# Attention and MLP in one kernel on one core: a fifth exp per slot into a stock of tiles before the tail

## The chip, the cores and the metric

One Trainium2 chip, one of its cores. The metric is the device time of one launch in microseconds, of which runs of the kernel before give 1628.36 to 1630.75, median 1630.4. "PE" is TensorE's matmuls, "PEld" its weight loads, "ACT" ScalarE, "DVE" VectorE, "POOL" GpSimd, "SP" the engine whose queue issues nearly all DMAs.

## The reference

The input x is 1 x 2048 x 512; attention has 32 heads of 16, the MLP 1792 hidden units, everything in float32.

```python
xn = _layernorm(x)
q, k, v = split(xn @ wqkv)                 # 32 heads of 16
p = softmax(q @ k.T * 16 ** -0.5)
s = (p @ v) @ wo
r = max(xn @ w1 + b1, 0)
g = silu((r * r) @ w2 + b2)
return x + s * g
```

## The kernel before

**Units, slots and lanes.** Attention is cut into 32 units (8 groups of four heads, times 4 blocks of 512 queries), a unit into 16 slots, one for each block of 128 keys: 512 slots, numbered through, run by one loop at the end of the function. For a slot's keys each of four heads needs one score matmul (`exp_mm`, line 1201, tile `se`, or `pm_t` if "spare") and one exp on ACT (line 1213) into a tile of the ring `pt`. At its end `pv_step` multiplies the exps of the slot two earlier with v into the bank `po` (line 401). Heads 0 and 2 use the upper 64 rows of the matmul array, heads 1 and 3 the lower; these halves are the lanes, and two matmuls on different lanes run side by side.

**Beside the exps.** The softmax needs each row's maximum before its exps. `max_mm` makes score matmuls 24 slots ahead (line 317, tile `pm_t`) and DVE reduces each (line 324). When a unit's maxima are complete, `shift` (lines 366 to 387) turns them on DVE, and DMAs on SP store them to `sh_d` one slot later (`keep`) and load them back into the unit's query tile `qe` (`back`), from where the score matmul subtracts them. The dense work (MLP, then the projection with wo) fills the other lane: `dense()` yields for each slot a list of matmuls, which `slot` interleaves with score matmuls by a string: "s" is an exp's matmul, "m" one for the maximum, "_" an empty place. The other lane's list is `own`.

**The projection.** From slot 454, `wo_part` multiplies 16 tiles of 128 rows with three quarters of wo: two slots each, nine matmuls on lane 0, then nine on lane 1 (line 223), all into the one bank `pd_t`; then ACT copies the bank out (line 736) and POOL gates the copy (lines 737, 738). Two waits bind the lanes: the first matmul of the next tile waits for the copy, and the first matmul of lane 1 waits for `last_use`, the exp or maximum issued last in the slot of lane 0. Per slot there are four exps, those of two key blocks for the two heads of the other lane. In 484 and 485 (PAIR) there are fewer maxima. From 486 (LAST_MAX), the tail, the maxima are through: `wo_last` adds the last quarter, three matmuls a slot, and exps fill the rest, five in one slot and three in the next, to two PSUM pools in turn (`odd`); DVE gates the bank (lines 759, 760).

**The end of a unit.** `evac` copies `po` out on ACT and in six steps, `EVAC` or `EVAC_LAST` slots later, takes the sums by DMA, inverts them (DVE), sends them to DRAM and back (`hl<-r_d`), multiplies and splits (POOL), and stores to `on_d`. Units 30 and 31 are handled on the chip (`unit_inner`, `unit_final`). All five engines follow the order in which the program is written; SP issues its DMAs in that order and stops at the first one that has to wait.

Of the kernel before, what the change touches and what calls it, by code (L numbers as in the profile page):

```python
# [33 lines left out]
NVT = 7  # L34
EVAC = (1, 6, 7, 9, 11, 14)
EVAC_LAST = (1, 3, 4, 5, 7, 9)
# [4 lines left out]
LAST_MAX = 486  # L41
PAIR = (484, 485)
# [12 lines left out]
def kernel(  # L55
# [56 lines left out]
    with ExitStack() as ph:  # L112
# [253 lines left out]
        def shift(u):  # L366
# [14 lines left out]
            def back():  # L381
                for p in range(2):
                    for i in range(2):
                        shift_rows(u, p, i)

# [3 lines left out]
        to_block = []  # L389

# [253 lines left out]
        def wo_pools():  # L644
            wos["f"] = right(wstk, "fp", 4)
            wos["oc1"] = right(wstk, "oc1p", 1)
            tp = tail["p"] = right(wstk, "tailp", 1)
            wos["oc3"] = right(o3, "oc3p", 2)

        def wo_small():  # L650

            tp = tail["p"]
            rows = tp.tile([P, D], F32, name="raw6")
# [3 lines left out]
            raw = tp.tile([P, D], F32, name="raw7")  # L657
            nc.gpsimd.memset(raw, 0.0)
            both = tp.tile([P, D], F32, name="raw67")
# [10 lines left out]
        def wo_load(c, kos):  # L670
            if len(kos) > 1:
                oc = wos["oc3"].tile([P, 2, len(kos), 512], F32R, name="oc")
            else:
                oc = right(wstk, f"oc1{c}p", 1).tile([P, 2, 1, 512], F32R, name="oc") if c else wos["oc1"].tile([P, 2, 1, 512], F32R, name="oc")

            def load(n, ko, a, b):
                nc.sync.dma_start(
                    oc[:, :, n, a:b].bitcast(F32),
                    on_d[ko][:, :, c * 512 + a : c * 512 + b].rearrange("k p t -> p k t"),
                )  # L680
# [10 lines left out]
        def wo_terms(ps, oc, tt, kos):  # L691
            wot = wos["w"]
            ts_ = slice(tt * P, (tt + 1) * P)
            return terms3(ps, [
                (lambda a, q, n=n: oc[q, a, n, ts_], lambda b, q, ko=ko: wot[q, b, ko])
                for n, ko in enumerate(kos)
            ])

        def wo_ask(k):
# [8 lines left out]
            elif c < 2:  # L708
# [6 lines left out]
        def wo_part():  # L715
            for c in range(4):
                for tt in range(4):
# [12 lines left out]
                    if c > 1:  # L730
                        s = tail[c, tt] = tail["p"].tile([P, D], F32, name=f"ts{c}{tt}")
# [3 lines left out]
                    def post():  # L735
# [3 lines left out]
                        if c < 2:  # L739
# [4 lines left out]
        def wo_last(c):  # L744
            for tt in range(4):
# [6 lines left out]
                if k == 18:  # L752
# [33 lines left out]
        def unit_turn(po, i):  # L786

            t = tail["p"].tile([P, 256], F32, name=f"tt{i}")
            nc.vector.transpose(t, po[:, 256 * i : 256 * i + 256])
            sm = tail["p"].tile([P, 8], F32, name=f"tsm{i}")  # L790
            return t.rearrange("p (b r) -> p b r", r=32), sm

        def unit_back(i, rows, sm):
            ot = tail["p"].tile([P, 256], F32, name=f"tot{i}")
# [4 lines left out]
            nc.vector.transpose(ot, rows.rearrange("p b r -> p (b r)"))  # L799
            return ot  # L800
# [38 lines left out]
        def unit_final(po):  # L839
# [5 lines left out]
            hls, ots = [], []  # L845
            for i in range(2):
                ot = unit_back(i, *unit_turn(po, i))
                hl = tail["p"].tile([P, 2, 256], F32R, name=f"thl{i}")
                nc.scalar.activation(hl[:, 0], ot, AF.Copy)
                hls.append(hl)  # L850
                ots.append(ot)

            def low(i):
                nc.vector.tensor_tensor(
                    hls[i][:, 1], ots[i], hls[i][:, 0].bitcast(F32), op=ALU.subtract
                )
# [13 lines left out]
            def add(tt, a, b, eng, queue):  # L870
                g, s = parts[tt]
                eng.tensor_tensor(g[:, a:b], g[:, a:b], s[:, a:b], op=ALU.add)
                queue.dma_start(of[1536 + tt * P : 1536 + (tt + 1) * P, a:b], g[:, a:b])

            low(0)
            for tt, n in ((0, 0), (0, 1), (1, 0), (1, 1), (0, 2), (1, 2)):
                out(tt, n)
            low(1)
            for tt in (2, 3):
                for n in range(3):  # L880
                    out(tt, n)
            gate(0)
            add(0, 0, D, nc.gpsimd, nc.scalar)
            gate(1)
            add(1, 0, D, nc.gpsimd, nc.scalar)
            gate(2)
            gate(3)
            add(2, 0, D, nc.vector, nc.sync)
            add(3, 0, D, nc.vector, nc.sync)

# [522 lines left out]
        def dense():  # L1413
# [12 lines left out]
            for c in range(3):  # L1426
                if c == 0:
                    o3.close()
                    wos["q6"] = right(wstk, "q6p", 1)
                    later(3, lambda: load_q6(3))  # L1430
                yield from wo_last(c)

        odd = itertools.chain((0,) * 4, itertools.cycle((1, 0)))
        flip = [0]
        seen = const.tile([P, 1], F32, name="seen")

        def slot(st, mms, post):
# [4 lines left out]
            for kb in (kb0, kb0 + 1):  # L1442
                pts.setdefault(kb, {})
            spare = st >= LAST_MAX
            ex = [
                lambda j=j, kb=kb: exp_mm(kb, j, pts[kb], spare and next(odd))
                for kb in (kb0, kb0 + 1) for j in (1 - lane, 3 - lane) if j not in pts[kb]
# [15 lines left out]
            if spare and lane == 0:  # L1463

                own.append(lambda: exp_mm(kb0, 0, pts[kb0], next(odd)))
# [11 lines left out]
            other = [None if o == "_" else (ex if o == "s" else mx).pop(0) for o in order]  # L1477
            other[-1:-1] = [None] * (len(own) - len(other))
# [54 lines left out]
        def plain_slot(st):  # L1533

            pts[st] = {}
            for j in range(4):
                exp_mm(st, j, pts[st], next(odd))
# [74 lines left out]
```

## Time and profile before

| | |
|---|---|
| timed runs | 1628.36, 1630.4, 1630.75 us |
| profiled execution | 1627.99 us, span 1626.2 us |
| PE busy | 1610.3 us, 99% of the span |
| DVE, ACT, POOL busy | 1362.1, 1188.9, 520.5 us |
| granted TensorE clock | 0.999 |
| slots 454 to 485 | up to about 1559 us, 3.27 us each |
| slots 486 to 511 | about 1559 to 1614 us |

The page gives the chain that ended last and the costliest groups. Rows of a timeline give the start, the length, the engine, the line, out<-in, the number of merged instructions and, in brackets, the idle time before and what ended it; a row of the windows gives start:end, its length, then busy us and instructions of PE, PEld, DVE, ACT and POOL, the clock, the DMA share and GB/s. An ACT or DVE row of several instructions runs from the first start to the last end.

### The profile page before, as it was taken

What the parts mean: (1) busy time and instruction counts of PE and PEld (TensorE: products, weight loads), DVE (VectorE), ACT (ScalarE), POOL (GpSimd) and SP (SyncE); (2) the same over time, 40 slices, a digit from 0 to 9 for tenths busy, and PEclk for the clock granted to TensorE, in tenths of its full rate; (3) what the DMA queues carried; (4) which work ended last, traced back from release to release, by engine and by line L of the source; (5) the groups of instructions that cost most, each with busy time, mean ns of one, the idle gap of its engine ahead of it and who ended that gap; (6) DMA issues with size and microseconds to landing.
All of it is one profiled execution on the core that took longest, in us unless ns stands there. A gap on an engine that the chain in (4) does not pass through costs nothing.

```text
span 1626.2 us, 36026 instructions
## 1 busy us (share of the span) xinstructions
PE 1610.3 (99%) x13656; PEld 936.1 (58%) x13656; DVE 1362.1 (84%) x2359; ACT 1188.9 (73%) x2349; POOL 520.5 (32%) x547
## 2 busy tenths in 40 slices
PE   8999999999999999999999999999999999999998
PEld 6899665556545654664466456545654565445543
DVE  6486888888888888888888888888888888887744
ACT  7212777777777777877777777777777777777786
POOL 6436667133113310321133112311331133226421
PEclk9999999999999999999999999999999999999999
DMA  8877556434343333434343334423542252247564
GB/s 297 235 236 233 175 162 157 127 96 128 81 103 96 103 88 90 127 87 110 83 119 93 85 87 130 112 68 83 141 112 67 70 155 78 55 126 210 188 179 150
DMA packets 163565, 208.16 MB, mean 128 GB/s; under 512 B 59168, under 2 KB 79136, under 8 KB 161824
## 3 DMA queue, kind: packets, MB, share of 16 engines
q1 hardware_dynamic: 163104, 205.33, 44.6%
q8 instruction: 108, 1.77, 0.5%
q14 instruction: 65, 0.53, 0.1%
q10 hardware_dynamic: 288, 0.52, 0.1%
HBM read 148.64 MB, written 55.56 MB: 126 GB/s over the span
## 4 chain that ended last, share of the span: by engine, by line
PE 98%; DVE 1%; DMA 0%; issue 0%; SPq 0%; DVEq 0%; ACT 0%; ACTq 0%
PE po L401 31%; PE pd_t L255 20%; PE pm_t L317 16%; PE se L1201 14%; PE pd_t L223 7%; PE pm_t L1077 4%; PE pd_t L1077 1%; PE se L1047 1%; PE se L981 1%; PE se L317 1%; PE pm_t L1163 0%; PE pd_t L1047 0%; DVE mx L324 0%; DMA xt<-in_A_x_dram 0%; PE pm_t L1201 0%; PE po L981 0%
## 5 line engine op out<-in xcount | busy, mean ns | idle before, releaser
L324 DVE TENSOR_REDUCE mx<-pm_t 128x1 f32<-128x512 f32 x1927 | 1197.3, 684 | 166.9 <-PE pm_t L317 74.0
L1213 ACT ACTIVATE pt<-se 128x512 f32<-128x512 f32 x1996 | 1035.5, 614 | 252.8 <-PE se L1201 210.4
L317 PE MATMUL pm_t<-ka,qm 64*128 64x512 f32 x1927 | 769.6, 420 | 0.0
L1201 PE MATMUL se<-qe,ka 64*128 64x512 f32 x1996 | 673.0, 396 | 0.3 <-ACT pt L1213 0.3
L401 PE MATMUL po<-pt,v 128*32 128x512 f32 x4096 | 545.3, 604 | 0.2 <-DVE tsm L795 0.2
L317 PEld LDWEIGHTS pm_t<-ka,qm 64*128 64x128 f32 x1927 | 338.3, 184 | 237.0 <-DVE mx L324 225.5
L1201 PEld LDWEIGHTS se<-qe,ka 64*128 64x128 f32 x1996 | 337.2, 184 | 18.1 <-ACT pt L1213 1.7
L255 PEld LDWEIGHTS pd_t<-xc,w1s 64*128 64x128 f32 x2352 | 292.0, 186 | 82.2 <-issue 82.2
L255 PE MATMUL pd_t<-xc,w1s 64*128 64x256 f32 x2352 | 332.2, 288 | 0.0
L255 PE MATMUL pd_t<-w2t,hT 64*128 64x512 f32 x1080 | 300.6, 410 | 0.0
L255 PEld LDWEIGHTS pd_t<-w2t,hT 64*128 64x128 f32 x1080 | 179.0, 184 | 83.2 <-issue 75.5
L555 POOL TENSOR_TENSOR r<-r 128x512 f32<-128x512 f32 x56 | 58.2, 1039 | 370.3 <-ACT r L552 370.3
L401 PEld LDWEIGHTS po<-pt,v 128*32 128x32 f32 x4096 | 81.0, 108 | 159.9 <-issue 136.8
L574 POOL TENSOR_TENSOR u<-u,b_t 128x512 f32<-128x512 f32 x16 | 20.6, 1289 | 320.2 <-ACT u L573 286.3
L324 DVE TENSOR_REDUCE mx<-se 128x1 f32<-128x512 f32 x121 | 77.9, 686 | 26.0 <-PE se L317 26.0
L439 POOL TENSOR_TENSOR ot<-ot,hl 128x512 f32<-128x512 f32 x30 | 38.6, 1286 | 173.9 <-DMA hl<-r_d 132.7
L223 PE MATMUL pd_t<-wot,oc 64*128 64x512 f32 x336 | 90.2, 405 | 0.4 <-issue 0.3
L552 ACT ACTIVATE r<-pd_t,b_t 128x256 f32<-128x256 f32 x112 | 47.0, 470 | 57.0 <-PE pd_t L255 53.8
L223 PEld LDWEIGHTS pd_t<-wot,oc 64*128 64x128 f32 x336 | 58.4, 184 | 46.9 <-ACT pt L1213 12.6
L1077 PE MATMUL pm_t<-xT,wr_t 64*128 64x512 f32 x408 | 73.8, 388 | 0.0
L97 POOL TENSOR_TENSOR hT<-r,hT 128x512 fp32r<-128x512 f32 x56 | 72.3, 1291 | 4.7
L223 PE MATMUL pd_t<-w2t,hT 64*128 64x512 f32 x264 | 68.8, 393 | 0.0
(134 smaller groups left out, 1148.4 us busy)
## 6 DMA issues: line engine op xcount, KB each, us to landing
w1s<-w_d SPq DMA_DIRECT2D x196, 256.0 KB
qm<-q_d SPq DMA_DIRECT2D x384, 32.0 KB
ka<-k_d SPq DMA_DIRECT2D x96, 128.0 KB
qe<-q_d SPq DMA_DIRECT2D x384, 32.0 KB
q_d<-hl SPq DMA_DIRECT2D x16, 512.0 KB
g<-g_d SPq DMA_DIRECT2D x32, 256.0 KB
k_d<-hl SPq DMA_DIRECT2D x15, 512.0 KB
hl<-r_d SPq DMA_DIRECT2D x30, 256.0 KB
```

What stands on the lines that cost most here:

```text
L97: (lo or nc.gpsimd).tensor_tensor(dst[1], raw, dst[0].bitcast(F32), op=ALU.subtract)
L223: mm = nc.tensor.matmul(out_, lh(r), rh(r), start=first_ and lane == 0, stop=last_ and lane == 1, skip_group_check=True,)
L255: mm = nc.tensor.matmul(out_, lh(r), rh(r), start=first_ and lane == 0, stop=last_ and lane == 1, skip_group_check=True,)
L317: nc.tensor.matmul(ps, qms[u][p][64 * j : 64 * j + 64, qb * P : (qb + 1) * P], kas[qd, p][64 * j : 64 * j + 64, kc * 512 : (kc + 1) * 512] ...
L324: return nc.vector.tensor_reduce(mxs[u][:, c, kc : kc + 1], ps, axis=AX.X, op=ALU.max)
L401: nc.tensor.matmul(po[32 * j : 32 * j + 32, :], vs[qd][:, (4 * kb + j) * VW : (4 * kb + j) * VW + 32], pts[j], start=(kb == 0), stop=(kb = ...
L439: nc.gpsimd.tensor_tensor(ot, ot, hl[:, 1].bitcast(F32), op=ALU.mult)
L552: nc.scalar.activation(r[:, i], ps[:, i * CW : (i + 1) * CW], AF.Relu, bias=b1_t[:, fo : fo + 1])
L555: nc.gpsimd.tensor_tensor(r, r, r, op=ALU.mult)
L1077: mm = nc.tensor.matmul(out_, lh(r), rh(r), start=first_ and lane == first, stop=last_ and lane != first, skip_group_check=True,)
L1201: nc.tensor.matmul(se, kas[qd, j // 2][b : b + 64, kb * P : (kb + 1) * P], qes[u][j // 2][b : b + 64, :], start=True, stop=True,)
L1213: return nc.scalar.activation(pts[j], se, AF.Exp, scale=0.25)
```

## The change

From slot 454 on (`RUN`) the exps of a slot are no longer those of its own two key blocks: `run_ahead` hands each lane the next exps in order, five a slot (six in PAIR, three in the tail), as long as their unit's shift has been issued and three tiles stay free. The ring gets 23 more tiles: 3 and 18 new ones and two slices of a v tile that is no longer used. The room comes from `wo_load`, which puts two of its three blocks into the free key tiles `ka`, and from the third row of partial results, which goes through DRAM (`sp_d`) like the first two. The fifth exp is put at the end of the slot's string. A slot without projection matmuls now issues only the exps that are due: none in 502, six in 511.

The rest concerns the tail: unit 31's shift is taken one slot after its maxima, not six; `EVAC_LAST`, which unit 29 alone uses, is shorter; a load of `on_d` is asked for one tile sooner; the last unit's scaling reads `po` again (`unit_scale`), its low parts are made on POOL, and one of the four last additions is done by PE with the identity and ACT.

```diff
+NXR = 18
-EVAC_LAST = (1, 3, 4, 5, 7, 9)
+EVAC_LAST = (1, 2, 2, 3, 4, 6)
+RUN = 454
...
-                late.append((g + (8 if u == 3 else 6 if u else 0), u))
+                late.append((g + {0: 0, 3: 8, NU - 1: 1}.get(u, 6), u))
...
+            more = [left.tile([P, 512], F32, name=f"xl{i}") for i in range(3)]
+            pool = right(wstk, "xpr", 1)
+            more += [pool.tile([P, 512], F32, name=f"xr{i}") for i in range(NXR)]
+            more += [vs["tiles"][0][:, 512 * i : 512 * i + 512] for i in range(2)]
+            rot["pt"] = more + rot["pt"]
...
+                two = rot["ka"][c % 2].rearrange("p (i k n) -> p i k n", i=2, k=2)
+                one = wos["oc3"].tile([P, 2, 512], F32R, name="oc")
+                oc = [two[:, :, 0], two[:, :, 1], one]
...
-                ot = unit_back(i, *unit_turn(po, i))
+                ot = unit_scale(po, i, *unit_turn(po, i))
+                nc.gpsimd.tensor_tensor(hl[:, 1], ot, hl[:, 0].bitcast(F32), op=ALU.subtract)
...
+            for tt in range(4):
+                gate(tt)
+            nc.tensor.matmul(both, ident, parts[1][0], start=False, stop=True)
+            nc.scalar.activation(parts[1][0], both, AF.Copy)
+            add(0, nc.gpsimd)
+            add(2, nc.gpsimd)
+            add(3, nc.vector)
...
+        def run_ahead(st, lane, n, need):
+
+            got = []
+            at = ahead_of.setdefault(lane, 2 * (st - 1))
+            live = sum(len(d) for d in pts.values())
+            while at < 2 * NU * 16:
+                kb, j = at // 2, lane + 2 * (at % 2)
+                if j not in pts.setdefault(kb, {}):
+                    if kb > need and (
+                        len(got) >= n or kb // 16 not in shifted or live + len(got) > len(rot["pt"]) - 3
+                    ):
+                        break
+                    assert kb // 16 in shifted
+                    got.append((kb, j))
+                at += 1
+            ahead_of[lane] = at
+            return got
...
+                n = 3 if spare else 6 if st in PAIR else 5
+                todo = run_ahead(st, 1 - lane, n, st - 1)
...
-            if spare and lane == 0:
-
-                own.append(lambda: exp_mm(kb0, 0, pts[kb0], next(odd)))
...
-                    order = "msmsmsms"
+                    order = "msmsmsms" + "s" * (len(ex) - 4)
...
+            elif k == 0 and not spare:
+                order += "s" * (len(ex) - 4)
             if st in PAIR:
-                order = "sms_s_s_m"
+                order = {5: "smss_ss_m", 6: "smssmss_s"}.get(len(ex), "sms_s_s_m")
...
+            last = st == NU * 16 - 1
+            todo = [run_ahead(st, lane, 0, st if last else st - 1) for lane in range(2)]
```

How it moves instructions is shown at three places; names end in the tile's number. First ACT around a tile's second slot (461), before: four exps (tiles pt0 to pt3), then the copy of `pd_t`, then the next slot's first exp.

```order
L1213 ACTIVATE pt0_1478<-se_21752 128x512 [waits PE_49,Activation_49]
L1213 ACTIVATE pt1_1479<-se_21760 128x512 [waits PE_49,Activation_49]
L1213 ACTIVATE pt2_1480<-se_21768 128x512 [waits PE_49,Activation_49]
L1213 ACTIVATE pt3_1481<-se_21776 128x512 [waits PE_49]
L736 ACTIVATE s_21712<-pd_t_21711 128x512 [waits PE_49]
L1213 ACTIVATE pt4_1482<-se_21805 128x512 [waits PE_49,Activation_49]
```

And ACT at the same place now: five exps (xr0 to xr4) ahead of the copy.

```order
L1232 ACTIVATE xr0_21448<-se_21890 128x512 [waits PE_49]
L1232 ACTIVATE xr1_21449<-se_21898 128x512 [waits PE_49,Activation_49]
L1232 ACTIVATE xr2_21450<-se_21906 128x512 [waits PE_49,Activation_49]
L1232 ACTIVATE xr3_21451<-se_21914 128x512 [waits PE_49]
L1232 ACTIVATE xr4_21452<-se_21922 128x512 [waits PE_49]
L748 ACTIVATE s_21845<-pd_t_21844 128x512
L1232 ACTIVATE xr5_21453<-se_21945 128x512 [waits PE_49,Activation_49]
```

The copy has moved one place back in ACT's queue. Second, PE at the end of a tile's first slot (462) and the start of its second (463), before: `oc` and `wot` are the projection's operands, `po` the four matmuls that end the slot.

```order
L223 MATMUL pd_t_21886<-wot_20339,oc_21586 128x512 [waits DMAHW5_49]
L317 MATMUL pm_t_21913<-ka3_735,qm1_205 128x512 [waits DVE_49]
L223 MATMUL pd_t_21886<-wot_20339,oc_21586 128x512 x2
L1201 MATMUL se_21918<-qe1_737,ka3_735 128x512 [waits Activation_49]
L401 MATMUL po_21384<-pt8_1486,v1_1789 32x512
L401 MATMUL po_21384<-pt4_1482,v1_1789 32x512
L401 MATMUL po_21384<-pt9_1487,v1_1789 32x512
L401 MATMUL po_21384<-pt5_1483,v1_1789 32x512
L223 MATMUL pd_t_21886<-wot_20339,oc_21586 128x512 [waits Activation_49]
L1201 MATMUL se_21934<-qe0_736,ka2_734 128x512
```

And PE there now, with `ka1` in place of a block of `oc`:

```order
L319 MATMUL pm_t_21965<-ka3_735,qm1_205 128x512 [waits DVE_49]
L225 MATMUL pd_t_21938<-wot_20339,oc_21623 128x512
L1220 MATMUL se_21969<-qe3_739,ka3_735 128x512 [waits Activation_49]
L225 MATMUL pd_t_21938<-wot_20339,oc_21623 128x512
L1220 MATMUL se_21973<-qe2_738,ka2_734 128x512 [waits Activation_49]
L405 MATMUL po_21384<-pt1_1479,v1_1789 32x512
L405 MATMUL po_21384<-pt13_1491,v1_1789 32x512
L405 MATMUL po_21384<-pt2_1480,v1_1789 32x512
L405 MATMUL po_21384<-pt14_1492,v1_1789 32x512
L225 MATMUL pd_t_21938<-wot_20339,ka1_208 128x512 [waits Activation_49]
```

The place beside the last projection matmul but one, empty before, holds an exp's matmul, and the exp for which the second slot's first matmul waits is now the slot's fifth. Third, PE at the start of slot 476, before: the exps' matmuls read `qe2` and `qe3`, the query tiles of unit 29.

```order
L223 MATMUL pd_t_22534<-wot_20339,oc_21880 128x512 [waits Activation_49]
L317 MATMUL pm_t_22537<-ka2_734,qm2_206 128x512 [waits DVE_49]
L223 MATMUL pd_t_22534<-wot_20339,oc_21880 128x512
L1201 MATMUL se_22541<-qe2_738,ka2_734 128x512
L223 MATMUL pd_t_22534<-wot_20339,oc_21880 128x512
L317 MATMUL pm_t_22545<-ka2_734,qm2_206 128x512 [waits DVE_49]
L223 MATMUL pd_t_22534<-wot_20339,oc_21880 128x512
L1201 MATMUL se_22549<-qe3_739,ka3_735 128x512
```

And PE there now: they read `qe0` and `qe1`, those of unit 30.

```order
L225 MATMUL pd_t_22612<-wot_20339,ka0_207 128x512 [waits Activation_49]
L319 MATMUL pm_t_22615<-ka2_734,qm2_206 128x512 [waits DVE_49]
L225 MATMUL pd_t_22612<-wot_20339,ka0_207 128x512
L1220 MATMUL se_22619<-qe0_736,ka2_734 128x512 [waits DMAHW6_49,DMAHW5_49,DMAHW7_49,DMAHW4_49,DMAHW3_49]
L225 MATMUL pd_t_22612<-wot_20339,ka0_207 128x512
L319 MATMUL pm_t_22623<-ka2_734,qm2_206 128x512 [waits DVE_49]
L225 MATMUL pd_t_22612<-wot_20339,ka0_207 128x512
L1220 MATMUL se_22627<-qe1_737,ka3_735 128x512 [waits DMAHW6_49,DMAHW5_49]
```

Unit 30's first exps have moved from slot 480 to slot 476, and their matmuls wait there for DMAs.

More of the change, by code (lines that the diff above doesn't have):

```diff
@@ L389 @@
         to_block = []
+        shifted = set()
         def shift_rows(u, p, i):
@@ L652, in wo_small @@
             tp = tail["p"]
-            rows = tp.tile([P, D], F32, name="raw6")
+            rows, raw, both = (tail[3, tt] for tt in range(3))
             nc.sync.dma_start(rows[64:], wo[(H - 8) * DH : (H - 4) * DH, :])
@@ L799, in unit_back, with unit_scale @@
             nc.vector.transpose(ot, rows.rearrange("p b r -> p (b r)"))
+            return ot
+        def unit_scale(po, i, rows, sm):
+            ot = tail["e"].tile([P, 256], F32, name=f"tot{i}")
+            nc.vector.reciprocal(sm, rows[:, :, DH])
+            nc.vector.transpose(
+                ot.rearrange("p (b r) -> p b r", r=32), sm[:, :, None].to_broadcast([P, 8, 32])
+            )
+            nc.vector.tensor_tensor(ot, po[:, 256 * i : 256 * i + 256], ot, op=ALU.mult)
             return ot
@@ L844, in unit_final @@
             parts = [wos.pop(28 + tt) for tt in range(4)]
-            hls, ots = [], []
+            both = pe.tile([P, 512], F32, name="se")
+            nc.tensor.matmul(both, ident, parts[1][1], start=True, stop=False)
+            hls = []
             for i in range(2):
-                ot = unit_back(i, *unit_turn(po, i))
-                hl = tail["p"].tile([P, 2, 256], F32R, name=f"thl{i}")
+                ot = unit_scale(po, i, *unit_turn(po, i))
+                hl = tail["e"].tile([P, 2, 256], F32R, name=f"thl{i}")
                 nc.scalar.activation(hl[:, 0], ot, AF.Copy)
+                nc.gpsimd.tensor_tensor(hl[:, 1], ot, hl[:, 0].bitcast(F32), op=ALU.subtract)
                 hls.append(hl)
[L851 to L856, printed above, removed]
             def out(tt, n):
@@ L1444, in slot @@
             spare = st >= LAST_MAX
+            if st < RUN:
+                todo = [
+                    (kb, j) for kb in (kb0, kb0 + 1) for j in (1 - lane, 3 - lane) if j not in pts[kb]
+                ]
+            else:
+                n = 3 if spare else 6 if st in PAIR else 5
+                todo = run_ahead(st, 1 - lane, n, st - 1)
             ex = [
-                lambda j=j, kb=kb: exp_mm(kb, j, pts[kb], spare and next(odd))
-                for kb in (kb0, kb0 + 1) for j in (1 - lane, 3 - lane) if j not in pts[kb]
+                lambda j=j, kb=kb: exp_mm(kb, j, pts[kb], (spare or st in PAIR) and next(odd))
+                for kb, j in todo
             ]
```

69 lines of the change are left out of this document (34 added, 35 removed).

## The prediction

> **What bounds the kernel now.** I read the chain that ended last on the page first, then the windows by stage, then the timelines of single engines from slot 454 on, where the order of instructions first differs.
>
> ```profile
> PE 98%; DVE 1%; DMA 0%; issue 0%; SPq 0%; DVEq 0%; ACT 0%; ACTq 0%
> ...
> 1450.00:1500.00 50.00, 50.00 (x382) 27.41 (x378) 38.63 (x67) 38.82 (x76) 27.85 (x25) 1.00 0.74 222
> ...
> 1550.00:1600.00 50.00, 49.05 (x365) 19.91 (x365) 23.93 (x49) 45.88 (x92) 10.95 (x11) 1.00 0.64 197
> ```
>
> TensorE is the chain, 98% of it, and never idle between 1450 and 1500 us; in the tail ACT fills up too (45.88 of 50). So an edit pays only where it shortens TensorE's queue, and costs wherever TensorE's next instruction comes to wait. Slots are counted back from the end: the last `po` group holds the steps of 509 to 511, and the step that ends slot st is that of st - 2. Two slots of the stretch before the tail (462 and 463) look like this:
>
> ```profile
> 1480.95 0.50 PE L223 MATMUL pd_t<-wot,oc 64*128 64x512 f32 x1
> ...
> 1483.22 1.07 PE L401 MATMUL po<-pt,v 128*32 128x512 f32 x8
> 1484.22 0.49 PE L223 MATMUL pd_t<-wot,oc 64*128 64x512 f32 x1
> ...
> 1486.17 0.39 PE L223 MATMUL pd_t<-wot,oc 64*128 64x512 f32 x1
> 1486.48 1.06 PE L401 MATMUL po<-pt,v 128*32 128x512 f32 x8
> 1487.48 0.50 PE L223 MATMUL pd_t<-wot,oc 64*128 64x512 f32 x1
> ```
>
> ```profile
> 1487.48 0.18 PEld L223 LDWEIGHTS pd_t<-wot,oc 64*128 64x128 f32 x1 [0.84 <-ACT s L736]
> ```
>
> ```profile
> 1481.79 2.17 ACT L1213 ACTIVATE pt<-se 128x512 f32<-128x512 f32 x4 [0.95 <-PE se L1201]
> 1484.82 2.07 ACT L1213 ACTIVATE pt<-se 128x512 f32<-128x512 f32 x4 [0.86 <-PE se L1201]
> 1486.74 0.63 ACT L736 ACTIVATE s<-pd_t 128x512 f32<-128x512 f32 x1
> ```
>
> Call the first of a projection tile's two slots A (1480.95) and the second B (1484.22). Each lasts 3.27 us: nine matmuls of the tile on one half of the array, eight others beside them, then the `po` step of 1.0. The third view is the point: the next tile's first weights wait for ACT's copy out of the one `pd_t` bank. That copy ends at 1486.74 + 0.63 = 1487.37, and the next tile starts at 1487.48. **The cover is 0.11 us.**
>
> **The change, part by part.** *The fifth exp.* On TensorE it is free: it stands in the ninth place beside the ninth tile matmul. ACT also has the room: 1577.07 to 1580.42 below are seven starts, 0.479 apart, so five exps and half a copy take 2.6 of 3.27.
>
> ```profile
> 1577.07 0.60 ACT L1213 ACTIVATE pt<-pm_t 128x512 f32<-128x512 f32 x1 [0.28 <-PE pm_t L1201]
> ...
> 1580.42 0.67 ACT L1213 ACTIVATE pt<-se 128x512 f32<-128x512 f32 x1
> ```
>
> What counts is the end of the slot, since ACT starts each slot idle and works through its exps one behind the other. In B the first exp starts 0.60 after the slot (1484.82 - 1484.22) and the copy four starts later (1486.74 - 1484.82 = 1.92). With five it starts at 0.60 + 5 x 0.479 = 3.00 and ends at 3.63; with 0.05 to wake TensorE (half the cover above) the next tile starts at 3.68 instead of 3.26: **+0.42**. In A the first exp starts at 0.84, the fifth at 2.76, and it ends 0.63 later (2.07 less three starts) at 3.39. The first tile matmul of B waits for the last exp of A (`last_use`), so B starts at 3.44 instead of 3.27: **+0.17**. Behind both waits stands all of TensorE's queue. Slots 454 to 483 are 15 such pairs; in 474 and 475 the order has only two exps each, so nothing is added there: 14 x 0.59 = 8.3. Slot 484 takes six exps, ending at 0.60 + 5 x 0.479 + 0.63 = 3.63: +0.4. Slot 485 keeps four. **Sum +8.7**; with no wake-up time 7.2, with the full 0.11 it is 10.4. Below nothing it cannot go: the nine tile matmuls stay.
>
> The Trainium skill, "ScalarE: Activation LUTs", section "Rules for kernel authors", gives about 0.3 us for an ACTIVATE and 0.83 ns per element: 0.73 for 512, an estimate. By it ACT would have 4.0 us of work in a slot of 3.27; the trace's 0.479 speaks against it.
>
> *Unit 30's shift.* The stock reaches unit 30's exps in slot 476 instead of 480. Their `qe` tile needs a round trip: shift on VectorE after slot 474, store to `sh_d`, load back.
>
> ```profile
> 1522.41 1.06 PE L401 MATMUL po<-pt,v 128*32 128x512 f32 x8
> ```
>
> ```profile
> 1523.56 0.19 DVE L371 SCALAR_TENSOR_TENSOR sh<-tr,sh 128x32 fp32r<-128x32 f32 x1
> ...
> 1579.71 0.69 DVE L759 TENSOR_TENSOR g<-pd_t,g 128x512 f32<-128x512 f32 x1 [2.05 <-DMA qe<-sh_d]
> ```
>
> ```profile
> 1473.13 0.45 SPq L377 DMA_DIRECT2D sh_d<-sh  x1
> ...
> 1477.84 2.09 SPq L392 DMA_DIRECT2D qe<-sh_d  x4
> ...
> 1525.71 0.38 SPq L377 DMA_DIRECT2D sh_d<-sh  x1
> ...
> 1531.41 2.11 SPq L392 DMA_DIRECT2D qe<-sh_d  x4
> ...
> 1577.14 2.12 SPq L392 DMA_DIRECT2D qe<-sh_d  x4
> ```
>
> ```profile
> L377 SPq DMA_DIRECT2D sh_d<-sh x4: 337/407/453, 1420.9 to 1572.5; - x4
> ...
> L392 SPq DMA_DIRECT2D qe<-sh_d x16: 473/479/542, 1423.9 to 1578.8; - x16
> ```
>
> Slot 475 starts at 1522.41 + 1.0 = 1523.41, the shift is done 0.34 later, and SP can store at 0.45 if nothing blocks it (before, it was blocked until 2.30). From store to load it took 4.7 (1473.13, and 1572.47 to 1577.14), 5.7 (1525.71) and 3.0 (1420.9 to 1423.9), and from the load to its landing 2.57 (1577.14 to 1579.71). So the tile is there at 0.45 + 4.7 + 2.57 = 7.7, and TensorE wants it in slot 476 at 3.27 + 0.34 = 3.6: **+4.1** of plain waiting, once. The ends: 2.4 with the trip of 3.0, 7.0 with before's own times (1531.41 + 2.57 - 1523.41 = 10.6). Before, four more slots hid it. Unit 29's shift stays hidden: its load went out at 1477.84 and lands about 1480.4; slot 462, where it is now wanted, starts at 1480.95 even before the delays of the pairs ahead of it.
>
> The Trainium skill, "DMA: Bandwidth & Descriptors", section "Anatomy of one DMA", gives some 2.0 us fixed for one DMA. By it the trip is 4.1 instead of 7.3 and this wait about 1; the trace's shortest first leg alone is 3.0.
>
> *Unit 31's shift* comes five slots sooner (end of 485), and its exps start in slot 490 instead of 496. On SP the load back stands behind the store of unit 29's output, which waits for GpSimd.
>
> ```profile
> 1553.01 0.32 SPq L428 DMA_DIRECT2D r_d<-sm  x1
> ...
> 1557.25 0.55 SPq L433 DMA_DIRECT2D hl<-r_d  x1
> ...
> 1567.14 1.73 SPq L448 DMA_DIRECT2D on_d<-hl  x4
> ```
>
> ```profile
> 1563.44 1.28 POOL L439 TENSOR_TENSOR ot<-ot,hl 128x512 f32<-128x512 f32 x1 [1.52 <-DMA hl<-r_d]
> ```
>
> EVAC_LAST asks for the reciprocals a slot sooner, but SP is issuing four loads until about 1551.5, so 1.5 us sooner. From there the rows' own distances: 4.2 to `hl`, 6.2 to GpSimd, 3.7 to the store, 1.75 of issue, 2.57 to land: 1570.0 on before's clock. Slot 490 starts 4 x 1.9 after slot 486 (1559.3), at 1566.9, and 1.0 later for the added waits of slots 482 to 485: **+2.1**. Ends 0 (only its own trip from about 1560: 1567.4) and 4.
>
> *The tail.* A spare slot held three or four places in a row, now three.
>
> ```profile
> 1558.34 1.06 PE L401 MATMUL po<-pt,v 128*32 128x512 f32 x8
> ...
> 1586.09 1.06 PE L401 MATMUL po<-pt,v 128*32 128x512 f32 x8 [0.23 <-DVE tsm L795]
> ...
> 1597.65 1.06 PE L401 MATMUL po<-pt,v 128*32 128x512 f32 x8
> ...
> 1599.77 1.06 PE L401 MATMUL po<-pt,v 128*32 128x512 f32 x8
> 1601.67 1.06 PE L401 MATMUL po<-pt,v 128*32 128x512 f32 x8
> ...
> 1611.36 3.03 PE L401 MATMUL po<-pt,v 128*32 128x512 f32 x24
> ```
>
> Four places are 2.12 (1597.65 to 1599.77), three 1.90. From 1558.34 to the end of the last `po` group it was 56.05. Now: 1.0 for the first step, 24 slots of 1.90, 1.0 for slot 502 that has no exp left, 1.13 for slot 511 with six exps, 3.03, and 0.45 in slot 498, whose `po` bank VectorE frees no sooner (it waited 0.23 with a place more): 52.2. **-3.9.** ACT has three exps in 1.90 and stops mattering.
>
> *The end.* VectorE loses two subtractions and one addition.
>
> ```profile
> 1618.18 0.43 DVE L854 TENSOR_TENSOR thl<-tot,thl 128x256 fp32r<-128x256 f32 x1 [0.17 <-ACT thl L849]
> 1618.60 1.89 DVE L868 TENSOR_TENSOR g<-pm_t,g 128x512 f32<-128x512 f32 x3
> ...
> 1621.01 2.02 DVE L872 TENSOR_TENSOR g<-g,ts 128x512 f32<-128x512 f32 x2
> ```
>
> The last addition ends at 1623.03. With the subtraction on GpSimd (about 0.8) the low part is there at 1618.95, two matmuls and two gates of 0.63 later it is 1620.8, one addition more 1621.5: **-1.4**, between -0.5 and -1.8.
>
> **Sum:** 8.7 + 4.1 + 2.1 - 3.9 - 1.4 = **+9.6**. The profiled run took 1627.99 (span 1626.2 and 1.8 around it), so 1637.6 on its terms. It lies below all three timed runs, whose mean is 1629.8 and median 1630.4; on the mean the forecast is **1639.4**.
>
> **The rivals.** *Only the handover costs* (0.15): SP has caught up, as its slots are longer, and both trips land in time: 8.7 - 5.3 = +3.4, 1633.2. For it: the 3.0 trip. Against: 4.7 and 5.7 where loads of `oc`, `g` and `xr` run beside it. *The waits stay covered* (0.12, the other side): the place is the first tile matmul of each slot. Spans of ACT overlap (0.63 long, 0.479 apart), so a bank may be free before its span ends; if a handover then costs under 5.3 / 28 = 0.19 and SP's longer slots hide both trips, the gain of 5.3 decides, and at no cost at all the time is 1624.5. Against: that copy's span is the last in its row, with nothing behind it to overlap, and its cover is 0.11. *Long trips* (0.15): before's own 7.0 and 4: 8.7 + 11.0 - 5.3 = +14.4, 1644.2. *ACT is the bound* (0.03): were the exps to run end to end at their spans of 0.63, A would end at 0.84 + 5 x 0.63 = 3.99 and the copy of B at 0.60 + 6 x 0.63 = 4.38, 0.77 and 1.17 late with the wake-up, 14 pairs of 1.94 or 27, and the time 1629.8 + 27 + 6.2 - 5.3 = 1657.7. Against: 0.479. The skill's figure named above would lead there. That the fifth exp isn't issued is excluded by the order.
>
> **How the numbers follow.** The forecast has 0.55. 0.2%, or 3.3 us, is about what a measurement of this kernel can tell from no change. Slower: 0.55, 0.15, 0.03 and half of the first rival, 0.80; same: its other half and a fifth of the second, 0.10; faster the rest, 0.10. The range takes in the first rival and the long trips with their handover a little dearer, 1632 to 1645.5; it leaves out the covered handover and the bound ACT, 0.15.
>
> **What would show it.** Right: weights of L223's line waiting on ACT's copy with TensorE idle about 0.4 in every B to A change and 0.17 in A to B, slots of 3.27 + 0.3 on average from 454 to 483; one idle stretch of some 4 us on TensorE in slot 476 released by the DMA `qe<-sh_d`, a second of 2 in slot 490; tail slots of 1.90. Wrong: if the pairs still take 6.53, the handover was covered, and if no stretch over 1 us ends at a DMA, the trips were hidden.

## The result and the profile after

The changed kernel takes 1642.78 us (median of six, 1641.21 to 1643.57), the kernel before beside it 1629.69 (1628.36 to 1632.3): a ratio of 1.0082, 95% interval 1.0072 to 1.0093, 13.1 us slower. The forecast was +9.6 and slower. The profiled execution has a span of 1640.7 us against 1626.2, +14.5 (before's lies 1.7 under its own median).

The chain by engine of the changed kernel, and the same two stretches in its windows:

```profile
PE 92%; ACT 2%; issue 2%; DMA 1%; POOL 1%; DVE 1%; SPq 1%; POOLq 0%; ACTq 0%; DVEq 0%
```

```profile
1450.00:1500.00 50.00, 48.11 (x370) 26.61 (x366) 36.28 (x63) 41.66 (x83) 25.97 (x24) 1.00 0.72 224
1550.00:1600.00 50.00, 45.73 (x328) 19.50 (x320) 24.12 (x44) 36.92 (x72) 13.72 (x11) 0.97 0.59 180
```

TensorE now stands 1.9 us of the first 50 and 4.3 of the second, and in the second the granted clock is no longer 1.00. Its waits from 1450 on (what waited, for what: us, times, longest):

```profile
PE pd_t L225 <- ACT s L748: 3.6, 11, 0.4
PE se L1220 <- DMA qe<-sh_d: 2.2, 2, 1.8
PE pm_t L1220 <- DMA qe<-sh_d: 2.1, 1, 2.1
PE pd_t L225 <- ACT ts L748: 1.0, 3, 0.3
PE se L1220 <- ACT xr L1232: 0.8, 1, 0.8
PE po L405 <- DVE tsm L807: 0.4, 1, 0.4
PE pd_t L225 <- ACT pt L1232: 0.4, 1, 0.4
```

All but the 0.8 on `xr` are in the forecast: the copy (`s` and `ts`), unit 30's load, unit 31's load, slot 498's `po` bank, and the last of slot 484's six exps (`pt`), for which slot 485 waits. A B slot and the A slot behind it, on TensorE and ACT:

```profile
1460.50 1.06 PE L405 MATMUL po<-xr,v 128*32 128x512 f32 x8
1461.85 0.49 PE L225 MATMUL pd_t<-wot,ka 64*128 64x512 f32 x1 [0.28 <-ACT s L748]
```

```profile
1458.75 2.56 ACT L1232 ACTIVATE xr<-se 128x512 f32<-128x512 f32 x5 [0.59 <-PE se L1220]
1461.15 0.65 ACT L748 ACTIVATE s<-pd_t 128x512 f32<-128x512 f32 x1
```

The copy starts 2.40 after the first exp (1.92 before) and ends at 1461.80; the next tile starts 0.05 later. To see where the time goes, I cut the stretch from slot 454 at the starts of the `po` steps (us; the slot that a step ends; "tail" runs to the end of the last `po` group):

| | 454-461 | 462-473 | 474-477 | 478-485 | tail | last `po` to span end |
|---|---|---|---|---|---|---|
| before | 26.15 | 39.19 | 13.06 | 26.13 | 56.05 | 11.8 |
| after | 27.83 | 42.87 | 17.99 | 28.84 | 58.00 | 11.4 |
| e1 copy first | 26.76 | 41.49 | 19.88 | 27.18 | 58.81 | 11.4 |
| e2 unit 30 sooner | 27.87 | 42.87 | 14.28 | 27.23 | 58.79 | 11.4 |
| e3 load first | 27.84 | 42.97 | 17.95 | 28.85 | 53.26 | 11.4 |
| e4 all three | 26.80 | 41.36 | 14.98 | 26.41 | 54.13 | 11.4 |
| e5 trips sooner | 26.76 | 46.29 | 13.44 | 26.41 | 53.98 | 11.4 |
| e6 tail and end | 26.80 | 45.83 | 13.45 | 26.43 | 53.22 | 12.4 |
| e7 copy late | 27.83 | 48.02 | 14.28 | 27.21 | 57.32 | 11.4 |
| e8 start later | 26.47 | 41.16 | 13.48 | 26.74 | 52.31 | 12.4 |
| e9 first exp sooner | 26.27 | 40.33 | 19.36 | 26.36 | 52.10 | 12.4 |
| e10 both | 26.24 | 41.07 | 13.22 | 26.31 | 53.09 | 12.4 |
| e11 start 460 | 26.26 | 40.19 | 13.20 | 26.63 | 52.43 | 12.4 |
| e12 best | 26.25 | 40.98 | 13.21 | 26.61 | 52.20 | 11.5 |

Single executions of one and the same front part reach slot 454 up to 2 us apart, so the stretches compare better than the spans.

### The profile page after: what moved, and what is told of

It reads as the page before. It is cut to its first block, busy times and chain, and to the rows that moved or that the text cites. A ratio compares the mean times of both kernels' runs of the same rounds, so it can differ in the third digit from the quotient of the medians.

```text
span 1640.7 us, 36050 instructions
## 1 busy us (share of the span) xinstructions
PE 1616.7 (99%) x13660; PEld 936.7 (57%) x13660; DVE 1361.2 (83%) x2356; ACT 1189.6 (73%) x2350; POOL 522.1 (32%) x549
## 4 chain that ended last, share of the span: by engine, by line
PE 92%; ACT 2%; issue 2%; DMA 1%; POOL 1%; DVE 1%; SPq 1%; POOLq 0%; ACTq 0%; DVEq 0%
PE po L405 29%; PE pd_t L257 19%; PE pm_t L319 16%; PE se L1220 14%; PE pd_t L225 5%; PE pm_t L1096 4%; PE se L1066 1%; PE pd_t L1096 1%; PE se L1000 1%; ACT pt L1232 1%; PE se L319 1%; ACT xr L1232 1%; DVE mx L326 0%; DMA g<-g_d 0%; PE pm_t L1182 0%
## 5 line engine op out<-in xcount | busy, mean ns | idle before, releaser
L1232 ACT ACTIVATE pt<-se 128x512 f32<-128x512 f32 x1892 | 975.1, 612 | 243.3 <-PE se L1220 203.3
L405 PE MATMUL po<-pt,v 128*32 128x512 f32 x3820 | 524.3, 605 | 0.0
L405 PEld LDWEIGHTS po<-pt,v 128*32 128x32 f32 x3820 | 77.6, 108 | 148.4 <-issue 125.8
L1096 PEld LDWEIGHTS pm_t<-xT,wr_t 64*128 64x128 f32 x408 | 58.8, 185 | 3.7
L225 PE MATMUL pd_t<-wot,ka 64*128 64x512 f32 x192 | 53.6, 410 | 5.0 <-ACT s L748 3.6
```

What stands on the lines that cost most here:

```text
L225: mm = nc.tensor.matmul(out_, lh(r), rh(r), start=first_ and lane == 0, stop=last_ and lane == 1, skip_group_check=True,)
L405: nc.tensor.matmul(po[32 * j : 32 * j + 32, :], vs[qd][:, (4 * kb + j) * VW : (4 * kb + j) * VW + 32], pts[j], start=(kb == 0), stop=(kb = ...
L1096: mm = nc.tensor.matmul(out_, lh(r), rh(r), start=first_ and lane == first, stop=last_ and lane != first, skip_group_check=True,)
L1232: return nc.scalar.activation(pts[j], se, AF.Exp, scale=0.25)
```

## The experiments

The theory: three separate costs (ACT's copy behind the fifth exp, unit 30's trip, unit 31's trip), less a gain in the tail. Rival one: ACT as a whole is short of time. Rival two: SP's queue and the DMA behind it are late whatever one asks. Medians, and ratios to the kernel before:

| run | us | ratio, 95% |
|---|---|---|
| after | 1642.78 | 1.0082 (1.0072 to 1.0093) |
| e1_copy_first | 1641.29 | 1.0074 (1.0058 to 1.0091) |
| e2_unit30_sooner | 1638.34 | 1.0059 (1.0044 to 1.0074) |
| e3_load_first | 1637.92 | 1.0055 (1.0040 to 1.0070) |
| e4_all_three | 1632.65 | 1.0024 (1.0014 to 1.0034) |
| e5_trips_sooner | 1636.07 | 1.0048 (1.0035 to 1.0061) |
| e6_best | 1635.0 | 1.0048 (1.0036 to 1.0059) |
| e7_trips_copy_late | 1641.41 | 1.0077 (1.0063 to 1.0092) |
| e8_start_later | 1628.64 | 1.0000 (0.9991 to 1.0009) |
| e9_first_exp_sooner | 1632.02 | 1.0019 (1.0009 to 1.0028) |
| e10_both | 1628.17 | 0.9996 (0.9987 to 1.0005) |
| e11_start_460 | 1627.85 | 0.9995 (0.9986 to 1.0004) |
| e12_end_back | 1626.56 | 0.9986 (0.9977 to 0.9995) |

**The copy ahead of the fifth exp (e1).**

```diff
+                if i == len(own) - 1 and not spare and st >= RUN and post is not None:
+                    post()
+                    post = None
                 if other[i] is not None:
                     follow = other[i]()
```

> From slot 454 on ACT gets the projection tile's copy ahead of the slot's fifth exp; TensorE's order is untouched. Theory (the copy comes late because it stands behind a fifth exp on ACT): the copy ends 0.48 sooner, TensorE's wait of 0.28 to 0.35 on it at each B to A change goes, the A slots fall from 3.7-3.8 back to 3.3-3.4, some 15 x 0.35 to 0.5 in all: 5 to 7 us less than the changed kernel, near 1636.5. Rival (ACT as a whole has too much to do with ten exps and a copy in a pair): the wait only moves from the copy to an exp bank or to the exp that the next tile's first matmul waits for, and the time stays within 2 us of 1642.8.

The time fell by only 1.5, as the rival had it, and yet the mechanism is the theory's. ACT in a B slot, and what TensorE still waits for:

```profile
1502.43 0.63 ACT L748 ACTIVATE s<-pd_t 128x512 f32<-128x512 f32 x1
1502.91 0.65 ACT L1232 ACTIVATE pt<-se 128x512 f32<-128x512 f32 x1
```

```profile
PE se L1220 <- DMA qe<-sh_d: 4.1, 2, 3.4
PE pm_t L1220 <- DMA qe<-sh_d: 1.8, 1, 1.8
```

The copy is ahead, every wait for it is gone, and A slots take 3.33 to 3.40 instead of 3.68 to 3.84. In the table that is -1.1, -1.4 and -1.7; but the wait for unit 30's load grew from 1.8 to 3.4 (474 to 477: +1.9), and slot 462 now waits for unit 29's load (+1.1, inside the -1.4). TensorE came to these loads sooner, and the loads did not. The tail is 0.8 longer for another reason. Its waits are shorter (1.8 and 0.6 instead of 2.1 and 0.8), but behind them the granted clock stays at half for 6.8 us, where in the changed kernel it does so for 3.4:

```profile
1581.00:1587.50 6.50, 6.12 (x25) 1.73 (x25) 1.52 (x3) 3.00 (x6) 0.00 (x0) 0.50 0.89 238
```

**Unit 30's shift sooner (e2), and unit 31's load first (e3).**

```diff
-{0: 0, 3: 8, NU - 1: 1}
+{0: 0, 3: 8, NU - 2: 2, NU - 1: 1}           # e2
-EVAC_LAST = (1, 2, 2, 3, 4, 6)
+EVAC_LAST = (1, 2, 2, 3, 4, 7)               # e3
```

> Unit 30's shift four slots sooner (end of slot 470). Its exps then also fill slots 474 and 475 (five each, not two), the stock is full from 480 on, and slots 480 to 485 hold four exps instead of five, five, five, five, six and four; the tail holds the same exps. Theory (slot 476 waits only for a trip that begins too late): the wait of 1.8 + 0.4 on the load and the 3.9 us that slots 476 and 477 are long go; one pair of handovers more (+0.6), two pairs and the six exps of 484 less (-2.0); -5.3, near 1637.5, a little less if unit 31's trip, whose chain now starts sooner against its slot, waits longer. Rival (SP and its queue are late in any case, so that the load also comes late when asked for sooner): a wait on the load of 2 to 4 us stays, in slot 474 or 475, and the time falls by at most 2.

> Unit 29's output is stored a slot later (the last entry of EVAC_LAST 7 instead of 6), so that on SP unit 31's load back stands ahead of it; no other engine's order changes. Theory (the load waits in SP's queue for GpSimd's result of unit 29): the load is issued about 3.0 us after its store, near 1576.2 instead of 1579.9, it lands about when slot 490 starts, and slots 490 and 491 lose 3.4 to 4.8 of their extra: near 1638.8. Rival (the trip's own latency, store and load, makes the wait): the load is issued no sooner than 1579, or lands 6 us after its issue, and the time falls by less than 1.

e2 is 4.4 faster: 474 to 477 lost 3.7 and 478 to 485 1.6, and the tail took back 0.8. The expectation allowed for that by a longer wait for unit 31, but the waits there add up to 3.0, against 2.9 before the edit; slots 490 to 492 take 1.2 more because the clock behind them stays at half for 6.8 us, as in e1, and slot 511 takes 0.4 less. e3 is 4.9 faster, all of it in the tail (58.00 to 53.26; slot 490 takes 1.96 instead of 5.52). SP's queue in the changed kernel and then in e3:

```profile
1562.83 0.38 SPq L432 DMA_DIRECT2D r_d<-sm  x1
1569.01 0.55 SPq L437 DMA_DIRECT2D hl<-r_d  x1
1573.04 0.32 SPq L379 DMA_DIRECT2D sh_d<-sh  x1
...
1578.10 1.73 SPq L452 DMA_DIRECT2D on_d<-hl  x4
1579.93 2.10 SPq L396 DMA_DIRECT2D qe<-sh_d  x4
```

```profile
1574.47 2.11 SPq L396 DMA_DIRECT2D qe<-sh_d  x4
1577.74 1.74 SPq L452 DMA_DIRECT2D on_d<-hl  x4
```

The load could go at 1574.5 and stood until 1579.9 behind a store that waited for GpSimd. The theory holds, for both.

**All three (e4).** The three diffs together.

> The three edits together: copy ahead of the fifth exp, unit 30's shift four slots sooner, unit 31's load ahead of unit 29's store. If the three waits are separate causes, their gains add up: the handovers left cost some 1 to 2 us, no wait over 0.5 us on a DMA is left on TensorE from slot 454 to 511, and the time is 1642.8 - 6 - 4.5 - 4 = about 1628, between 1626 and 1630, level with the kernel before or just under it. If they hide one another (an engine that is short of time behind all three), the sum is well short of that: over 1633.

-10.1, about the sum of the three (1.5 + 4.4 + 4.9), but not the 14.5 that the expectation gave them. Left are three waits for loads: in slot 462 (+1.0), 474 (+1.7) and 494 (1.65 for `oc<-on_d`).

**All loads sooner (e5), and the copy late again on top (e7).**

```diff
-NU - 2: 2, NU - 1: 1}
+NU - 3: 4, NU - 2: 0, NU - 1: 1}
-EVAC_LAST = (1, 2, 2, 3, 4, 7)
+EVAC_LAST = (1, 2, 2, 2, 4, 7)
```

> All three edits together, and the three waits for loads that are left there taken away too: unit 29's shift two slots sooner (slot 462 waited 0.5 and lost 1.0), unit 30's another two (slot 474 lost 1.7), and unit 29's sums brought back a slot sooner (a tail slot waited 1.65 for oc). Theory (what the copy's place saved was taken back by loads that come at their own time): all three waits go, no DMA wait over 0.3 us is left on TensorE after 1450, and the time falls by 1.0 + 1.7 + 1.7 = 4.4 to 1628.3 (1627 to 1629.5), about level with the kernel before. Rival (the loads are late because SP's queue is full, not because they are asked for late): waits of together over 2 us are left, at other slots, and the time stays over 1630.5.

> The kernel of e5_trips_sooner with ACT's copy behind the fifth exp again, as in the changed kernel; nothing else. Theory (the handover's own price is 0.35 to 0.45 in each of 13 B to A changes, and in e1_copy_first it was hidden by longer load waits): with no load wait to hide it, it is paid in full, 4.5 to 6 us more than e5_trips_sooner, near 1633.5. Rival (the handover is worth only the 1.5 us that moving the copy gained by itself): 1 to 2 us more.

The expectation of e5 failed: 3.4 slower than e4, not 4.4 faster. TensorE, and SP's own waits from 1458 to 1492:

```profile
1488.42 0.79 PE L225 MATMUL pd_t<-wot,oc 64*128 64x512 f32 x1 [3.67 <-DMA oc<-on_d]
```

```profile
SPq L396 <- DMA sh_d<-sh: 3.7, 1, 3.7
SPq L689 <- DMA hl<-r_d: 3.4, 1, 3.4
```

Asked for two slots sooner, unit 29's load back stands ahead of the loads of the last weights and of `oc`, and SP waits 3.7 us in front of it for the store to land. All behind it is 3.6 later (`oc<-on_d` at 1479.32, in e4 at 1475.69), and slot 462 waits for `oc`. So rival two is right at this place: SP is one row, and what is moved up in it pushes something else back. e7 is 5.3 slower than e5 (6.3 between the two profiled executions): 4.4 of it in the four stretches up to 485 (13 handovers of 0.34, the theory), its tail is another 3.3 longer by a wait for `oc`, and its part ahead of slot 454 happened to be 1.5 shorter.

**The tail and the end (e6).** A gap slot may take two exps per lane; the third last tile's residual goes through TensorE and ACT.

```diff
-todo = [run_ahead(st, lane, 0, ...
+todo = [run_ahead(st, lane, 0 if last else 2, ...
...
-            add(2, nc.gpsimd)
+                nc.tensor.matmul(both[tt - 1], ident, parts[tt][0], start=False, stop=True)   # tt = 1, 2
+                nc.scalar.activation(parts[tt][0], both[tt - 1], AF.Copy)
```

> e5_trips_sooner with the two terms of the tail and the end that came short: slot 502, which holds no exp, takes four, so that slot 511 has two instead of six; and the residual of the third last tile goes through TensorE and ACT like the second's, so that VectorE's last addition stands beside no GpSimd addition. Theory: slot 502 +0.5, slot 511 and the last po group -1.5, the last addition 0.7 instead of 1.26, -0.4 at the end: -1.4 against e5_trips_sooner, near 1627, under the kernel before by 1 to 3.5 us. Rival (the six exps' time on ACT is what counts, wherever they stand, and the end waits for the last stores): within 0.5 of e5_trips_sooner.

The ratio is the same as that of e5, so the expected 1.4 did not come. The first edit works: slot 502 took 0.8 more, slot 511 with the last `po` group 1.5 less. The second gives that back and more: VectorE's last addition does fall to 0.69, but the end is 0.9 longer (12.4 instead of 11.4). These rows are of e8's timeline and chain, which has the same end:

```profile
1621.65 0.69 DVE L891 TENSOR_TENSOR g<-g,ts 128x512 f32<-128x512 f32 x1
```

```profile
1615.87 1.91 PE se L868 x4
1620.52 1.80 PE se L902 x4
1622.34 0.60 ACT g L903
```

The changed kernel has this in its chain:

```profile
1630.82 1.05 PE se L867 x2
```

The second identity matmul makes 1.91 on TensorE out of 1.05, in front of the last products. Behind them the chain no longer ends on VectorE but with the closing identity matmuls (1.80) and ACT's copy (0.60): 2.4 from the last product, against 2.6 to the end of VectorE's addition in e12. So nearly all that VectorE saves is spent again, and the 0.9 stays.

**A later start (e8), and the order in the A slots (e9, e10, e11).**

```diff
-RUN = 454
+RUN = 458                                                        # e8, from e6; 460 in e11
-NU - 3: 4, NU - 2: 0, NU - 1: 1}, EVAC_LAST = (1, 2, 2, 2, 4, 7)
+NU - 2: 1, NU - 1: 1},            EVAC_LAST = (1, 2, 2, 3, 4, 7)  # e8; NU - 2: 2 in e9
-later(3, lambda: load_q6(3))
+later(6, lambda: load_q6(3))                                     # e8
-order = "msmsmsms" + "s" * (len(ex) - 4)
+order = ("smsmsmsm" if st >= RUN else "msmsmsms") + ...           # e9 to e11
-n = 3 if spare else 6 if st in PAIR else 5
+n = 3 if spare else 5                                            # e11
```

> e4_all_three with the fifth exp from slot 458 instead of 454 (the stock is full just before the tail, at 484 instead of 480, so no exp of it is lost, and units 29 and 30 are wanted a slot or so later), unit 30's shift one slot sooner than there, the load of q for the last tile three slots later (so that unit 29's oc has the queues to itself), and the tail and end edits of e6_best; unit 29's shift stays where the changed kernel has it, ahead of nothing on SP. Theory (a trip costs what SP and the DMA leave of its time, and asking sooner only helps where SP has nothing urgent behind it): the 4 us wait for oc of e5_trips_sooner does not come back, slot 462's 1.0 and 474's 1.7 fall under 0.5 together, the tail slot's 1.65 under 1, tail and end give 1.5: 1632.7 - 2.2 - 1 - 1.5 = 1628, between 1626.5 and 1629.5, level with the kernel before. Rival (SP's queue is full between 455 and 476, so one wait only goes into another): 1631 or more.

> e8_start_later with two edits. Unit 30's shift a slot later again, as in e4_all_three: in e8_start_later it fell into the slot whose maxima VectorE had just finished, TensorE waited 0.28 for a bank of theirs and the slot lost 0.65 to 0.75. And from slot 458 on the A slots begin with an exp where they began with a maximum, as the B slots do, so that ACT's row of five starts 0.23 sooner and the fifth exp's bank is free in time. Theory (in e8_start_later an A slot costs 0.07 more than a B slot because its fifth exp waits for a bank): A slots 3.33 instead of 3.40, 13 x 0.07 = -0.9, the shift -0.65, a wait of up to 0.5 for unit 30's load against it: 1627.4 beside 1628.6, at most just measurable. Rival (ACT still has the last exp of the B slot in hand when the A slot starts, so that an earlier exp only waits for ACT): A slots stay at 3.40, and the time at 1628 to 1629.

> e9_first_exp_sooner with unit 30's shift where e8_start_later had it, a slot sooner, ahead of the loads of ka and oc on SP; the A slots still begin with an exp. Theory (e9_first_exp_sooner took 0.05 to 0.1 off each slot from 458 on and lost 6.3 in slots 474 and 475 because the shift's store and load stood behind two big loads): slots of 3.28 to 3.30 as there, no wait of several us for unit 30, 0.65 lost where the shift meets the maxima; 1632.0 - 6.3 + 0.7 = 1626.5, 1.5 to 2.5 under the kernel before. Rival (a faster front only meets the next load, as in e1_copy_first): a wait of 2 us or more for a load somewhere from 462 to 495, and 1628 to 1630.

> e10_both with the fifth exp from 460 and five in 484 and 485 too, so that the stock of 34 is reached as the tail begins; unit 29 is wanted half a slot later. Theory: the 0.8 that slot 462 lost to unit 29's load in e9_first_exp_sooner goes, 484 and 485 lose 0.1 to 0.3: 1626, 0.5 under e10_both. Rival (the two slots with a pair of spare banks have no room for a fifth exp): 484 and 485 lose 0.4 each as slot 484 did in the changed kernel, and it is level with e10_both or slower.

e8 is as expected: no wait for unit 29, 30 or 31 is left, and it is level with the kernel before. e9 took the slots from 3.33 and 3.40 to 3.28 to 3.30, which is all but free, and still lost 3.4 against e8. SP, TensorE and the clock around slot 474 there:

```profile
1516.11 1.00 SPq L379 DMA_DIRECT2D sh_d<-sh  x1
...
1524.00 2.10 SPq L396 DMA_DIRECT2D qe<-sh_d  x4
```

```profile
1526.51 0.76 PE L1221 MATMUL se<-qe,ka 64*128 64x512 f32 x1 [3.00 <-DMA qe<-sh_d]
```

```profile
1526.00:1528.00 2.00, 1.49 (x5) 0.49 (x9) 0.00 (x0) 0.60 (x1) 0.00 (x0) 0.50 0.27 74
```

One slot later in SP's row, behind the loads of `ka`, `g` and `xr`, the store needs 7.9 us to the load back instead of 3.3 (1513.59 to 1516.88 in e8). With the shift a slot sooner again (e10), and the start at 460 (e11), the slots stay at 3.28 and the long wait is gone, but a wait of 1.3 for `oc` came back in e10, and both missed their expectations of 1626.5 and 1626: level with the kernel before.

**The best version (e12).** e11 with the end of the changed kernel.

> e11_start_460 with the end of the changed kernel again (GpSimd adds the third last tile's residual, one pair of identity matmuls on TensorE instead of two). Theory (the second pair of identity matmuls, 0.86 on TensorE ahead of the last products, cost more than VectorE's addition alone, 0.69 instead of 1.26, gave back): from the end of the last po group to the end of the span 11.4 to 11.5 instead of 12.4, so 1.0 less: 1626.9 beside 1629.0, 0.1% under the kernel before, the interval just short of or just beyond no change. Rival (the last stores set the end, whatever is added when): 12.2 or more, and level with e11_start_460.

1626.56, 0.14% under the kernel before, by an interval (0.9977 to 0.9995) that does not reach 1. All that TensorE waits for from 1450 on in it:

```profile
PE po L405 <- DVE tsm L807: 0.4, 1, 0.4
PE pd_t L225 <- issue: 0.4, 1, 0.4
PE pd_t L225 <- DMA oc<-on_d: 0.2, 1, 0.2
```

## Why the prediction was right, and where its steps were off

**Handover: forecast +8.7, measured about 9.1.** The pairs of 454 to 473 took 0.54 more, those of 478 to 483 0.61 (forecast 0.59); 474, 484 and 485 another 1.3, and 0.6, one pair's worth, is taken to lie in 476 and 477. The split was off: B to A 0.42 in the first slots and 0.54 from 462 on, A to B 0.06 instead of 0.17. e1, and e7 against e5, show the copy's place as the cause of 0.35 to 0.42 of each B to A change. The 0.05 to 0.1 a slot that e1 leaves goes when the A slots begin with an exp (e9 against e8). Starts of exps stayed 0.48 apart (2.56 for five, the last 0.64 long), so the bound ACT fell as a rival.

**Unit 30's trip: forecast +4.1, measured 3.9 (476 and 477 4.5 longer, less their handover), by other parts.** The store went out 0.4 after slot 475's start as forecast, but store to load took 3.0, the range's shortest (1529.52 to 1532.48), and the load 2.4 to land, so TensorE waited 2.2, not 4.1. (By the figure of the Trainium skill that the prediction quoted, "DMA: Bandwidth & Descriptors", section "Anatomy of one DMA", which fits it for DMAs issued from GpSimd, the wait would have been about 1, an estimate; neither leg of this trip was as short as 2.0.) The windows behind that wait hold the rest:

```profile
1533.00:1537.00 4.00, 1.81 (x13) 1.26 (x14) 1.56 (x3) 1.00 (x2) 3.75 (x5) 0.97 0.30 77
1537.00:1541.00 4.00, 4.00 (x23) 1.50 (x21) 1.23 (x3) 2.07 (x5) 1.11 (x1) 0.60 0.51 189
```

At a clock of 0.60 over 4 us TensorE loses 1.6, and 0.1 before. The forecast's size was right by accident: a trip reckoned too long stood for a clock that it did not know.

**Unit 31's trip: forecast +2.1, measured 5.2** (slots 490 to 492 took 10.85 instead of three times 1.89). This term failed by 3.1, most of the miss.

```profile
1582.39 0.47 PE L1220 MATMUL pm_t<-qe,ka 64*128 64x512 f32 x1 [2.11 <-DMA qe<-sh_d]
1583.68 0.46 PE L1220 MATMUL se<-qe,ka 64*128 64x512 f32 x1 [0.79 <-ACT xr L1232]
```

```profile
1584.00:1586.00 2.00, 2.00 (x11) 0.16 (x8) 0.16 (x1) 1.08 (x2) 0.00 (x0) 0.63 0.73 255
1586.00:1588.00 2.00, 2.00 (x14) 1.03 (x14) 0.26 (x1) 1.13 (x3) 0.00 (x0) 0.51 0.51 171
```

The wait for the load is 2.11, as forecast, by the chain that it named (e3). That it agrees to the tenth is luck: from `r_d` to `hl` it took 6.2 (1562.83 to 1569.01), not 4.2, and from there to GpSimd 5.4, not 6.2.

```profile
1574.41 1.28 POOL L443 TENSOR_TENSOR ot<-ot,hl 128x512 f32<-128x512 f32 x1 [6.49 <-DMA hl<-r_d]
1582.90 0.60 ACT L1232 ACTIVATE xr<-pm_t 128x512 f32<-128x512 f32 x1 [2.85 <-PE pd_t L225]
```

Priced at nothing were the 0.79 that TensorE then waits for ACT, which had run dry with it (idle for 2.85), and the clock: (1 - 0.63 + 1 - 0.51) x 2 = 1.7. With 2.11 that is 4.6; what the other 0.6 is, no row here shows. The whole price was 1.8 times what TensorE waited, 5.2 for 2.9; behind unit 30's load it was 3.9 for 2.2.

**The tail: forecast -3.9, measured -3.2** (58.00 - 5.2 - 56.05). The slots of 1.90 and slot 498's 0.5 came as forecast. Slot 511 did not: from its start to the end of the last `po` group it took 5.1, not 4.2.

```profile
1625.62 3.62 PE L405 MATMUL po<-pt,v 128*32 128x512 f32 x24
```

```profile
1627.49 0.65 ACT L1232 ACTIVATE pt<-se 128x512 f32<-128x512 f32 x1
```

The forecast counted the six exps as places on TensorE; with nothing beside them they go at ACT's 0.48 each, and the last `po` steps wait for the one that ends at 1628.14. With two exps there, e12 has the -3.9 (52.20).

**The end: forecast -1.4, measured -0.4.** (The forecast's own times, 1621.5 and 1623.03, give -1.5.) From the last `po` step to the last addition it is 0.7 less, the stores 0.4 more.

```profile
1635.88 1.26 DVE L890 TENSOR_TENSOR g<-g,ts 128x512 f32<-128x512 f32 x1
```

```profile
1635.32 1.26 POOL L890 TENSOR_TENSOR g<-g,ts 128x512 f32<-128x512 f32 x1 [0.21 <-DVE g L886]
```

The one addition left takes 1.26, not 0.7, beside one on GpSimd; alone it takes 0.69 (e8). It stood until GpSimd's ended at 1636.58, and then needed 0.56. (The Trainium skill, "SBUF — State Buffer", section "SBUF: two separate sides", says of the port pair that VectorE with two SBUF inputs shares with GpSimd that whichever starts first holds it for its whole instruction and the other blocks; these rows agree.)

Summed: 9.1 + 3.9 + 5.2 - 3.2 - 0.4 = 14.6, against 14.5 in the spans and 9.6 in the forecast. Of the rivals, the covered handover and "only the handover costs" are out by these rows; "long trips" came nearest in time, but by the clock, not by the trips. What the sum did not see at all is that its terms are not independent: take the 5 us of handover away, and longer waits for loads and the clock behind them take 3.8 back (e1).

## What to carry to other kernels

Where one engine is the bound and several loads come just in time, a saving ahead of them becomes a longer wait for them, so mend the loads first and read a single edit's worth slot by slot, not from the total. A DMA queue that stops at the first waiting entry is a row of its own in the sum: before an entry is asked for sooner, list what then stands behind it. And of two operations that feed a bound engine, issue the one whose buffer it wants next (the copy of the only bank) ahead of the one that is only stock.

## What the runs showed of the hardware beyond that

A wait of over 2 us costs TensorE more than the wait. Behind each of those from 1450 on that lasted 2.2 us or more, in one piece or two close together, the granted clock fell to 0.50: for 3.4 us behind slots 476 (2.2) and 490 (2.9) of the changed kernel, for 6.8 in e1 (3.4 and 2.4), e2 (3.0) and e9 (3.0). After 1.65 (slot 494 of e4) it stayed at 1.00:

```profile
1582.00:1584.00 2.00, 1.64 (x14) 0.70 (x14) 0.16 (x1) 1.10 (x3) 0.00 (x0) 1.00 1.06 392
1584.00:1586.00 2.00, 2.00 (x18) 0.64 (x14) 0.69 (x1) 1.66 (x4) 0.00 (x0) 1.00 1.05 402
```

The Trainium skill, "TensorE: Matmul & The Clock Gate", section "Part 1: The HAM clock gate", has the clock halve after at least one idle window of about 3.4 us and come back after a busy one. The traces agree on the half clock and, in slot 476, on some 3.4 us until it is back (1.7 lost at half speed), though it was twice that in e1, e2 and e9; idle stretches of 2.2 us were already enough here.

The same store and load back of a shift (`sh_d`) took 3.0 us from issue to issue in the changed kernel and 7.9 in e9, where loads of `ka`, `g`, `xr` and again `ka` had gone out on SP just ahead of it.
